# Grouped-query decode block: query-stationary score matmuls, transposed softmax weights, and a rearranged load schedule

## The chip, the cores and the metric

The kernel runs on one core of a Trainium2 chip. The metric is the device time of one execution in microseconds (us), median of several runs. Ratios in this text are the mean time of one kernel's runs over that of the other kernel's runs of the same rounds, with a 95% interval; they are therefore not quite the ratio of the medians quoted next to them. A difference between two variants that were timed in different rounds is a difference of their medians; it is good to some 0.5 us.

## The reference

One decoding step of a transformer block with adaptive layer norm. Batch and query length are 1, the cache holds 65536 positions, and everything is bfloat16.

```python
mod = (silu(c) @ w_mod)                       # 6 x 512: shifts, scales, gates
h = layernorm(x) * (1 + ca) + sa
q = h @ wq                                    # 32 query heads of 128
scores = einsum(q, k) * 128 ** -0.5           # 8 KV heads, 4 query heads share one
p = softmax(scores);  o = einsum(p, v)        # k_cache, v_cache: 8 x 65536 x 128
x = x + ga * (o @ wo)
h = layernorm(x) * (1 + cb) + sb
x = x + gb * ((silu(h @ w_gate) * (h @ w_up)) @ w_down)
```

K and V are 134 MB each. Every byte is used once, so the kernel is a stream of 285.5 MB through one core.

## The kernel before

K and V are loaded in 2 MB chunks of 64 tokens per partition (16 KB per partition), 8 chunks a head, in four K buffers and four V buffers. K loads run 10 chunks ahead of V loads, because V can be used only when a head's softmax is done.

```python
kbuf = ctx.enter_context(tc.tile_pool(name="kbuf", bufs=4))
vbuf = ctx.enter_context(tc.tile_pool(name="vbuf", bufs=4))
LAG = NCH + max(2, NCH // 4)                  # 10 chunks
...
def k_group(g, cidx, j, kt):                  # 8 tokens per partition
    tp = ps_t.tile([P, NPAIR, P], F32, ...)
    for pi in range(NPAIR):                   # two bf16 tokens seen as one fp32 row: 4 transposes
        src = kt[:, t0 : t0 + 2, :].bitcast(F32).rearrange("p a b -> p (a b)")
        nc.tensor.transpose(tp[:, pi, :], src, ident_f[:])
    ktT = ktp.tile([P, NPAIR, P], F32, ...)   # copied by ACT and DVE in turn
    ...
    def emit_s(...):                          # K is the stationary operand
        for pi in range(NPAIR):
            for e in range(2):
                nc.tensor.matmul(sp[:, rep * tl : rep * tl + SN], lhsT=kv[:, :, e], rhs=QB[e][:, g], ...)
...
# softmax of a head: strided max over the free axis, all-reduce over partitions (POOL),
# then four strided exps; only after all four may the head's first V matmul start
...
def v_chunk_start(g, cidx):
    if cidx == 0:
        wo_g = wop.tile([P, rep, D], BF16, ...)
        nc.sync.dma_start(out=wo_g[:], in_=A_wo[...])       # 512 KB in rows of 1 KB
    vt = vbuf.tile([P, CH, Dh], BF16, ...)
    nc.sync.dma_start(out=vt[:], in_=v_src(g, cidx))
...
# after the last V chunk: w_gate, w_up, and w_down in rows of 1 KB, 13/14 of it and then 1/14
```

All large loads are issued by the sync engine (SP) on one queue, in program order; each is spread over the 16 DMA engines.

## Time and profile before

| | before |
|---|---|
| time, median | 688.67 us (687.31 to 689.43, 5 runs) |
| profiled span | 686.9 us |
| input queue (q1) | 285.49 MB, 98.3% of the 16 engines' time |
| PE busy | 524.5 us, 76% |

The page of the kernel before: busy times, then the granted PE clock in tenths and GB/s in 40 equal slices of 17.2 us, then two DMA queues with packets, MB and share of the 16 engines' time.

```profile
span 686.9 us, 17142 instructions
PE 524.5 (76%) x7730; PEld 434.7 (63%) x7730; DVE 253.3 (37%) x420; ACT 194.4 (28%) x324; POOL 12.8 (2%) x40
...
PEclk9999979987999789998999979997899979997555
...
GB/s 350 428 426 405 410 426 429 428 428 421 429 428 428 427 431 426 428 428 425 430 427 430 425 428 432 426 427 424 432 428 427 428 423 430 430 427 424 366 427 192
...
q1 hardware_dynamic: 25488, 285.49, 98.3%
q8 instruction: 60, 0.98, 0.5%
```

The rate is flat near 428 GB/s. The slices below 428 are where to look, and the windows of busy time make them sharper (us from the span's start, length, then busy us of PE, PE weight loads, DVE, ACT and POOL with instruction counts, granted PE clock, DMA share, GB/s):

```profile
60.00:80.00 20.00, 19.36 (x324) 18.82 (x321) 12.85 (x16) 8.91 (x15) 0.00 (x0) 1.00 0.98 394
...
635.00:645.00 10.00, 4.18 (x48) 1.45 (x49) 0.18 (x1) 5.09 (x8) 0.48 (x2) 0.59 0.79 329
...
670.00:680.30 10.30, 5.73 (x137) 4.99 (x135) 2.73 (x15) 0.20 (x2) 0.60 (x1) 0.50 0.81 308
680.30:686.90 6.60, 2.02 (x56) 1.93 (x56) 0.33 (x2) 0.00 (x0) 0.00 (x0) 0.50 0.01 0
```

The largest PE groups (line, engine, operation, out<-in, shapes, count; busy us, mean ns, idle before):

```profile
L268 PE MATMUL tp<-ident_f,k 128*128 128x128 f32 x2048 | 325.5, 294 | 13.4 <-DMA k<-in_A_k_cache_dram 13.3
L283 PE MATMUL sp<-qb,ktT 128*128 128x64 bf16 x4096 | 213.9, 197 | 83.3 <-ACT ktT L273 64.5
...
L316 PE MATMUL oacc<-v,pt 128*16 128x512 bf16 x1024 | 96.0, 410 | 29.1 <-DMA v<-in_A_v_cache_dram 20.9
```

The end of the chain of waits (start, length, what): loads, until the larger piece of w_down lands at 680.25 (the small one lands at 680.55), then all 56 w_down matmuls, then the output.

```profile
628.96 18.77 DMA v<-in_A_v_cache_dram
...
651.09 29.16 DMA wd<-in_B_w_down_dram
680.25 0.05 issue
680.29 2.04 PE pd L422 x56
```

### The profile page before, as it was taken

To read this page: it belongs to the slowest core of one execution; us is meant where nothing else is said; L and a number is where in the kernel's file an instruction comes from. 1 tells how busy PE (TensorE), PEld (TensorE's weight loads), DVE (VectorE), ACT (ScalarE), POOL (GpSimd) and SP (SyncE) were. 2 spreads that over 40 slices of the span, in tenths; PEclk is the share of its full clock that TensorE was granted. 3 is DMA by queue.
4 is the path that set the end of the run, shared out by engine and by line. 5 is a ranking of instruction groups with operands and counts; after the bars stand their busy time and mean duration, and the time that the engine had idled before them with its cause. 6 is when DMAs were issued, how large, how long until landed. Compare 5 with 4: busy or idle time off the path is not lost.

```text
span 686.9 us, 17142 instructions
## 1 busy us (share of the span) xinstructions
PE 524.5 (76%) x7730; PEld 434.7 (63%) x7730; DVE 253.3 (37%) x420; ACT 194.4 (28%) x324; POOL 12.8 (2%) x40
## 2 busy tenths in 40 slices
PE   2699849975999489975998469974999739984344
PEld 2699847864777378864776358863877637772114
DVE  1255714451434234351433324432443514433001
ACT  0144343324233323324232143323232232320200
POOL 1000000000000000000000000000000000000000
PEclk9999979987999789998999979997899979997555
DMA  9999999999999999999999999999999999999895
GB/s 350 428 426 405 410 426 429 428 428 421 429 428 428 427 431 426 428 428 425 430 427 430 425 428 432 426 427 424 432 428 427 428 423 430 430 427 424 366 427 192
DMA packets 25849, 286.58 MB, mean 417 GB/s; under 512 B 2736, under 2 KB 8624, under 8 KB 8624
## 3 DMA queue, kind: packets, MB, share of 16 engines
q1 hardware_dynamic: 25488, 285.49, 98.3%
q8 instruction: 60, 0.98, 0.5%
q14 instruction: 13, 0.11, 0.0%
q10 hardware_dynamic: 288, 0.00, 0.0%
HBM read 285.48 MB, written 0.00 MB: 416 GB/s over the span
## 4 chain that ended last, share of the span: by engine, by line
PE 47%; DMA 27%; issue 13%; DVE 6%; ACT 6%; POOL 1%; SPq 0%; POOLq 0%; ACTq 0%
PE tp L268 25%; DMA v<-in_A_v_cache_dram 15%; PE sp L283 13%; PE oacc L316 7%; DMA k<-in_A_k_cache_dram 7%; DMA wd<-in_B_w_down_dram 4%; ACT pt L238 4%; DVE mx L230 4%; ACT ktT L273 2%; DVE sc L287 1%; PE pa L349 1%; DVE osb L336 1%; DVE oacc L298 0%; SPq L118 0%; DVE ktT L275 0%
## 5 line engine op out<-in xcount | busy, mean ns | idle before, releaser
L268 PE MATMUL tp<-ident_f,k 128*128 128x128 f32 x2048 | 325.5, 294 | 13.4 <-DMA k<-in_A_k_cache_dram 13.3
L283 PE MATMUL sp<-qb,ktT 128*128 128x64 bf16 x4096 | 213.9, 197 | 83.3 <-ACT ktT L273 64.5
L283 PEld LDWEIGHTS <-ktT 128*128 128x128 bf16 x4096 | 186.2, 101 | 129.7 <-ACT ktT L273 67.3
L273 ACT ACTIVATE ktT<-tp 128x512 f32<-128x512 f32 x256 | 153.0, 598 | 381.9 <-PE tp L268 381.9
L268 PEld LDWEIGHTS tp<-ident_f,k 128*128 128x128 f32 x2048 | 234.9, 149 | 26.4 <-issue 23.6
L275 DVE COPY ktT<-tp 128x1024 bf16<-128x1024 bf16 x256 | 176.1, 691 | 148.1 <-PE tp L268 145.8
L316 PE MATMUL oacc<-v,pt 128*16 128x512 bf16 x1024 | 96.0, 410 | 29.1 <-DMA v<-in_A_v_cache_dram 20.9
L287 DVE COPY sc<-sp 128x256 f32<-128x256 f32 x64 | 27.1, 424 | 178.0 <-PE sp L283 178.0
L316 PEld LDWEIGHTS <-pt 128*16 128x16 bf16 x1024 | 25.3, 91 | 53.9 <-issue 30.2
L238 ACT ACTIVATE pt<-sc,nb 128x512 bf16<-128x512 f32 x32 | 40.7, 1422 | 58.1 <-POOL nb L235 58.1
L230 DVE TENSOR_REDUCE mx<-sc 128x4 f32<-128x2048 f32 x8 | 30.4, 3805 | 0.2
L150 PE MATMUL pmod<-scT,wm 128*128 128x1 bf16 x96 | 3.3, 172 | 12.8 <-DVE scT L144 12.8
L233 POOL PARTITION_ALL_REDUCE gmx<-mx x8 | 3.1, 383 | 464.2 <-DVE mx L230 464.2
L150 PEld LDWEIGHTS <-wm 128*128 128x128 bf16 x96 | 3.4, 118 | 12.7 <-DMA wm<-in_w_mod_dram 7.2
L336 DVE COPY osb<-oacc 128x512 f32<-128x512 f32 x7 | 4.8, 692 | 15.8 <-PE oacc L316 15.8
L339 PE MATMUL pT<-ident_f,osb 128*128 128x128 f32 x32 | 6.2, 323 | 5.3 <-DVE osb L336 4.8
L333 DVE COPY osb<-oacc 128x256 f32<-128x256 f32 x1 | 0.4, 425 | 24.7 <-PE oacc L316 24.7
L249 DVE RECIPROCAL linv<-lt 128x4 f32<-128x4 f32 x8 | 1.4, 176 | 21.8 <-POOL lt L247 21.7
L349 PEld LDWEIGHTS <-wo 128*128 128x128 bf16 x128 | 4.9, 118 | 6.5 <-DVE obf L345 6.5
L339 PEld LDWEIGHTS pT<-ident_f,osb 128*128 128x128 f32 x32 | 3.8, 158 | 7.9 <-DVE osb L336 6.3
L349 PE MATMUL pa<-obf,wo 128*128 128x1 bf16 x128 | 5.5, 173 | 4.2 <-DVE obf L345 4.2
L334 ACT ACTIVATE osb<-oacc 128x256 f32<-128x256 f32 x1 | 0.4, 384 | 29.5 <-DVE osb L333 29.5
(66 smaller groups left out, 58.7 us busy)
## 6 DMA issues: line engine op xcount, KB each, us to landing
k<-in_A_k_cache_dram SPq DMA_DIRECT2D x64, 2048.0 KB, 24.4
v<-in_A_v_cache_dram SPq DMA_DIRECT2D x64, 2048.0 KB, 27.7
wq<-in_A_wq_dram SPq DMA_DIRECT2D x2, 2048.0 KB, 17.5
wo<-in_A_wo_dram SPq DMA_DIRECT2D x8, 512.0 KB, 28.5
wm<-in_w_mod_dram SPq DMA_DIRECT2D x2, 1536.0 KB, 8.5
wg<-in_B_w_gate_dram SPq DMA_DIRECT2D x1, 1792.0 KB, 21.4
wu<-in_B_w_up_dram SPq DMA_DIRECT2D x1, 1792.0 KB, 25.2
wd<-in_B_w_down_dram SPq DMA_DIRECT2D x1, 1664.0 KB, 29.2
```

The source lines that it names most:

```text
L150: nc.tensor.matmul(pmod[:, k * DC + cco : k * DC + cco + 1], lhsT=strided_cols(wrow(wm_pieces, cci)[:, k * D : (k + 1) * D], DC, cco), rhs ...
L230: nc.vector.reduce_max(out=mx[:], in_=sc_g[:].rearrange("p (t h) -> p h t", h=rep), axis=AX.X)
L238: nc.scalar.activation(out=pt_th[:, :, h], in_=sc_th[:, :, h], func=AF.Exp, bias=nb[:, h : h + 1], scale=scale, accum_out=lsum[:, h : h + 1],)
L268: nc.tensor.transpose(tp[:, pi, :], src, ident_f[:])
L273: nc.scalar.activation(out=ktT[:], in_=tp[:], func=AF.Identity)
L275: nc.vector.tensor_copy(out=ktT[:].bitcast(BF16), in_=tp[:].bitcast(BF16))
L283: nc.tensor.matmul(sp[:, rep * tl : rep * tl + SN], lhsT=kv[:, :, e], rhs=QB[e][:, g], start=(e == 0), stop=(e == 1))
L287: nc.vector.tensor_copy(out=sc_g[:, c0 * CH * rep : (c0 + SPC) * CH * rep], in_=sp[:, 0 : SPT * rep])
L316: nc.tensor.matmul(oacc[32 * jg : 32 * jg + 4 * rep, :], lhsT=pt_g[:, rep * t : rep * (t + 4)], rhs=vt[:, tl : tl + 4, :], start=(t < RT), ...
L336: nc.vector.tensor_copy(out=osb[:], in_=oacc[:])
L339: nc.tensor.transpose(pT[:, ib, :], osb[:, ib * Dh : (ib + 1) * Dh], ident_f[:])
L349: nc.tensor.matmul(pa[:, cco : cco + 1], lhsT=strided_cols(wo_g[:, hh, :], DC, cco), rhs=o_bf[:, hh : hh + 1], start=(hh == 0), stop=(hh = ...
```

## The change

q becomes the stationary operand of the score matmuls (32 columns, four column tiles next to each other, 512 moving columns), so scores come out head by head on partitions; the softmax then works on contiguous rows, and its weights P are transposed on PE for the V matmuls. Seven of the eight wo loads move into the phase in which only K is loaded. After the last K chunk every second V chunk goes into a freed K buffer. w_down is loaded in 2 KB rows and four pieces. One transpose buffer in PSUM is given up for P. And one small unused tile is added at the top.

```diff
+    pad = const.tile([P, 40], F32, name="pad")
+    nc.gpsimd.memset(pad[:], 0.0)
...
-    wop = ...(name="wop", bufs=2)          # ktp 6, ps_t 4, SLAG 2
+    wop = ...(name="wop", bufs=max(2, Hkv - 1))   # ktp 7, ps_t 3, ps_p 1, SLAG 1
...
-                for e in range(2):
-                    nc.tensor.matmul(sp[:, rep * tl : rep * tl + SN], lhsT=kv[:, :, e], rhs=QB[e][:, g], ...)
+        quad.append((cidx * NG + j, ktT))
+        if len(quad) == 4: ...
+                for e in range(2):
+                    for gidx, ktT_m in members:
+                        nc.tensor.matmul(sp[32 * jg : 32 * jg + 32, :], lhsT=QBk[e][:, g, k, :],
+                            rhs=kv[:, :, :, e], ..., tile_position=(0, 32 * jg))
...
+        nc.vector.reduce_max(out=mx[:], in_=sc_g[:], axis=AX.X)
+        for blk in range(NBLK):
+            nc.scalar.activation(out=p_sb[:], in_=sc_g[:, blk * BW : (blk + 1) * BW], func=AF.Exp, ...)
+            for pp in range(4):
+                nc.tensor.transpose(ptps[:, pp, :], p_sb[:, pp * P : (pp + 1) * P], ident_bf[:])
+            nc.vector.tensor_copy(out=ptT[:, blk], in_=ptps[:])
...
-        vt = vbuf.tile([P, CH, Dh], BF16, name=f"v{g}_{cidx}", tag="vbuf")
+        late = g * NCH + cidx + LAG - Hkv * NCH
+        if late >= 0 and late % 2 == 0:
+            vt = kbuf.tile([P, CH, Dh], BF16, name=f"v{g}_{cidx}", tag="kbuf")
+        else:
+            vt = vbuf.tile([P, CH, Dh], BF16, name=f"v{g}_{cidx}", tag="vbuf")
...
+            if 1 <= step <= Hkv - 1:
+                load_wo(step - 1)            # the eighth follows the last V chunk
...
-        wd_v = B_w_down.rearrange("(c p) n -> p c n", p=P)
+        wd_v = B_w_down.rearrange("(c p e) n -> p c e n", p=P, e=2)
+        for c0, c1 in ((0, 2), (2, 4), (4, 6), (6, FC // 2)):
...
```

## The prediction

> **What bounds the kernel now.** The DMA engines. The page's slice row shows 417 GB/s over the span and about 428 in nearly every slice; the SP queue's 285.5 MB take 98.3% of the 16 engines' time. At 428 GB/s they cost 667 us; about 20 us of the 686.9 us span is not steady streaming. Busy times by window place most of it:
> - 0 to 10 us: 224 and 359 GB/s, 3.2 us lost (the start).
> - 60 to 80 us: 370 to 406 GB/s, 1.6 us lost. Only K is loaded; PE is 97% busy. The chain shows 0.47 (transposes) + 0.23 (scores) = 0.70 us per group of 8 K tiles, 5.6 us a chunk, against 4.9 us for the DMA to bring one.
> - 635 to 645 us: 329 GB/s, 2.3 us lost. The last softmax (max 3.8 us, then nearly 9 us until POOL scales it, four exps 5.1 us) holds the first V matmul until 640; the four V buffers are full.
> - 670 to 680.3 us: 308 GB/s, 2.9 us lost: the skewed end, and w_down in 1 KB rows. 1 KB packets take 46 ns, 16 KB ones 611 ns: 22 against 27 bytes per ns and engine.
> - 680.3 to 686.9 us: 6.6 us without input. The chain shows 2.04 us of w_down matmuls after the last landing, then the output.
>
> In between, the 4+4 buffers absorb the stalls of PE (76% busy), DVE and ACT.
>
> **What the change does.**
> - Scores: q becomes the 32-column stationary operand, four column tiles side by side: 1024 matmuls of 512 columns replace 4096 of 64 with a 128x128 weight load each. The V matmuls have this form already; twelve take 0.76 us in the chain, 0.063 us each. Estimate: 0.13 us per group, not 0.23. The Trainium skill ("TensorEngine Tiling (Array Packing)", Key Properties) says tiles run loads and matmuls in parallel; the 0.063 us agrees.
> - Added: 128 transposes of P, copies, mask algebra. The transposes wait in PE order on the softmax: a stall of about 10 us per head, like ACT's stall today (longest PE wait 10.4 us). The buffers should absorb it.
> - wo loads move into the K-only phase, same bytes; each gives PE 1.5 us of slack there.
> - Late V chunks alternate into freed K buffers: the 635 us starvation goes.
> - w_down in 2 KB rows, four pieces: estimate 0.5 us less DMA; only 8 of 56 matmuls wait for the last piece, 1.7 us less.
> - About a third fewer instructions: the instruction queue (0.5%, 3.5 us of DMA time) shrinks about 1 us.
>
> **On the critical path.** The PE work that shrinks (scores, 214 us busy) is hardly critical. Gain: 1.6 + 2.3 + 0.5 + 1.7 + 1 + 0.4 (smoother end) = 7.5 us, about 1%.
>
> **Prediction:** 681 us, range 677 to 686.5. Faster by over 2%: 3%; within 2%: 94%; slower: 3%. Over 2% needs 674.9, about the floor of 667 + 3 + 5.
>
> **Right if:** PE busy falls to roughly 400 us or less, or its clock does, with DMA still at 428 GB/s in the middle slices; no dip at 60 to 80 us, none after the last K chunk; under 5.5 us from the last landing to the end; the chain of waits mostly DMA.
>
> **Wrong if:** PE, on a lower clock because it idles more, can't catch up after each softmax stall, so that K buffers stay full (slices below 420 repeating every 80 us); three transpose buffers or the quad bursts throttle the K-only phase; the late wo load delays the last head so that gu, not w_down, ends last (today gu is 1.1 us ahead of w_down).

## The result, and the profile after

The changed kernel takes 681.9 us (681.47 to 682.01, 7 runs), the kernel before 688.16 us in the same and earlier rounds (13 runs). The ratio is 0.9906 (0.9896 to 0.9916): about 6.3 us, 0.9%. Executions over 1.5% slower than the fastest of the same kernel are left out of the means.

The page of the changed kernel:

```profile
span 680.2 us, 11269 instructions
PE 504.9 (74%) x4786; PEld 329.5 (48%) x4786; DVE 245.7 (36%) x451; ACT 188.3 (28%) x340; POOL 14.2 (2%) x45
...
GB/s 347 425 419 417 431 431 430 430 430 430 429 427 431 426 429 430 431 429 428 431 430 430 431 428 430 428 430 428 427 429 430 430 431 431 429 429 431 416 424 210
...
q1 hardware_dynamic: 24624, 285.49, 99.0%
q8 instruction: 37, 0.61, 0.3%
```

The dips of 405 and 410 have become 417 and 431, the 366 near the end has become 416, and the plateau stands at 430. PE busy fell by 20 us only, and its mean granted clock went from 0.894 to 0.88. The same windows and groups:

```profile
60.00:80.00 20.00, 19.76 (x160) 12.96 (x159) 9.27 (x14) 7.76 (x13) 0.00 (x0) 1.00 1.02 423
...
630.00:645.00 15.00, 7.92 (x99) 3.92 (x93) 2.81 (x11) 0.43 (x2) 0.44 (x1) 0.73 1.01 415
640.00:645.00 5.00, 1.88 (x16) 0.54 (x16) 0.00 (x0) 0.00 (x0) 0.00 (x0) 0.50 1.00 380
...
664.00:674.60 10.60, 6.61 (x167) 5.89 (x165) 2.72 (x15) 0.18 (x1) 0.60 (x1) 0.50 0.76 308
674.60:680.20 5.60, 1.06 (x24) 0.95 (x24) 0.33 (x2) 0.00 (x0) 0.00 (x0) 0.50 0.02 1
```

```profile
L297 PE MATMUL tp<-ident_f,k 128*128 128x128 f32 x2048 | 289.3, 296 | 73.6 <-DMA k<-in_A_k_cache_dram 45.2
...
L317 PE MATMUL sp<-ktT,qbk 128*32 128x512 bf16 x1024 | 137.3, 419 | 1.6 <-ACT ktT L302 0.3
L375 PE MATMUL oacc<-v,ptT 128*16 128x512 bf16 x1024 | 92.6, 422 | 24.4 <-DMA v<-in_A_v_cache_dram 24.4
```

A small dip remains after the last K chunk, 380 GB/s at 640 to 645 us. It is not starvation: the DMA share is 1.00, and 18 of the 116 packets of 16 KB that start there take 0.8 to 1.4 us in place of 0.61. Why they do is open.

The chain now ends with a wait for w_down and only 24 of its matmuls:

```profile
656.19 18.44 DMA wd<-in_B_w_down_dram
674.63 0.05 issue
674.67 1.07 PE pd L483 x24
```

### Two readings made from the trace's DMA records

GB/s in slices tells an average over 16 engines. Two more readings, worked out from the records of DMA packets and landings, proved more useful.

The first is **when** so many MB of the input queue had been moved (us from the span's start; the ends of the packets, added up):

| MB moved | before | changed | difference |
|---|---|---|---|
| 20 | 50.58 | 51.04 | +0.46 |
| 40 | 99.50 | 98.21 | -1.29 |
| 120 | 287.20 | 285.12 | -2.07 |
| 260 | 615.69 | 611.91 | -3.78 |
| 272 | 646.24 | 639.93 | -6.31 |
| 285.4 | 679.03 | 673.84 | -5.19 |

Each column comes from one profile, and such times scatter. Two variants below, late_v_only and wd_only, run the program of the kernel before without any difference until after the last K chunk; their profiles have 98.84 and 98.34 us at 40 MB and 614.94 and 614.45 us at 260 MB. A lead of about 1 us in a single profile therefore shows nothing.

The second is the **spread**: each load raises its semaphore 16 times, once per DMA engine, so the trace shows when the first and the last of the 16 engines finished a given load. "Last input" is the last landing of any load.

| kernel | instruction packets (q8) | spread near 100 / 300 / 620 us | last input | span | last input to end |
|---|---|---|---|---|---|
| before | 60 | 2.7 / 5.3 / 11.2 | 680.6 | 686.9 | 6.3 |
| changed | 37 | 2.2 / 4.7 / 8.1 | 675.3 | 680.2 | 4.9 |

The engines do not advance together. They drift apart all through the run, to 11 us in the kernel before and to 8 us in the changed one. A load counts as landed when its slowest engine is done, so the engine that is furthest behind decides the end.

### The profile page after: what moved, and what is told of

Same layout as the page of the kernel before. It is cut to its first block, busy times and chain, and to the rows that moved or that the text cites. A ratio compares the mean times of both kernels' runs of the same rounds, so it can differ in the third digit from the quotient of the medians.

```text
span 680.2 us, 11269 instructions
## 1 busy us (share of the span) xinstructions
PE 504.9 (74%) x4786; PEld 329.5 (48%) x4786; DVE 245.7 (36%) x451; ACT 188.3 (28%) x340; POOL 14.2 (2%) x45
## 4 chain that ended last, share of the span: by engine, by line
PE 39%; DMA 37%; issue 12%; DVE 7%; ACT 2%; SPq 1%; POOL 1%; POOLq 0%; DVEq 0%; ACTq 0%
DMA k<-in_A_k_cache_dram 23%; PE tp L297 21%; PE sp L317 9%; DMA v<-in_A_v_cache_dram 9%; PE oacc L375 5%; DMA wq<-in_A_wq_dram 3%; DMA wd<-in_B_w_down_dram 3%; DVE mx L247 2%; DVE ktT L304 2%; PE ptps L269 2%; SPq L424 1%; ACT p L259 1%; ACT sc L331 1%; DVE osb L395 1%; PE pa L408 1%
## 5 line engine op out<-in xcount | busy, mean ns | idle before, releaser
L297 PE MATMUL tp<-ident_f,k 128*128 128x128 f32 x2048 | 289.3, 296 | 73.6 <-DMA k<-in_A_k_cache_dram 45.2
L317 PE MATMUL sp<-ktT,qbk 128*32 128x512 bf16 x1024 | 137.3, 419 | 1.6 <-ACT ktT L302 0.3
L375 PE MATMUL oacc<-v,ptT 128*16 128x512 bf16 x1024 | 92.6, 422 | 24.4 <-DMA v<-in_A_v_cache_dram 24.4
L317 PEld LDWEIGHTS <-qbk 128*32 128x32 bf16 x1024 | 31.8, 95 | 55.7 <-issue 47.5
L375 PEld LDWEIGHTS <-ptT 128*16 128x16 bf16 x1024 | 27.9, 91 | 48.4 <-issue 32.5
L269 PE MATMUL ptps<-ident_bf,p 128*128 128x128 bf16 x128 | 16.2, 266 | 38.3 <-ACT p L259 38.3
L259 ACT ACTIVATE p<-sc,nb 128x512 bf16<-128x512 f32 x32 | 22.9, 716 | 49.5 <-DVE nb L255 45.5
L247 DVE TENSOR_REDUCE mx<-sc 128x1 f32<-128x2048 f32 x8 | 18.3, 2286 | 15.0 <-ACT sc L331 15.0
L270 DVE COPY ptT<-ptps 128x512 bf16<-128x512 bf16 x32 | 13.6, 424 | 25.0 <-PE ptps L269 24.5
L329 DVE COPY sc<-sp 128x512 f32<-128x512 f32 x16 | 11.1, 691 | 16.2 <-PE sp L317 16.2
```

What stands on the lines that cost most here:

```text
L247: nc.vector.reduce_max(out=mx[:], in_=sc_g[:], axis=AX.X)
L259: nc.scalar.activation(out=p_sb[:], in_=sc_g[:, blk * BW : (blk + 1) * BW], func=AF.Exp, bias=nb[:, 0:1], scale=scale, accum_out=lblk[:, b ...
L269: nc.tensor.transpose(ptps[:, pp, :], p_sb[:, pp * P : (pp + 1) * P], ident_bf[:])
L270: nc.vector.tensor_copy(out=ptT[:, blk], in_=ptps[:])
L317: nc.tensor.matmul(sp[32 * jg : 32 * jg + 32, :], lhsT=QBk[e][:, g, k, :], rhs=kv[:, :, :, e], start=(k == 0 and e == 0), stop=(k == 3 and ...
L329: nc.vector.tensor_copy(out=sc_g[:, blk * BW : (blk + 1) * BW], in_=sp[:])
```

## The experiments

Theory A is that of the prediction: the queue is the limit, and the gain is the sum of stretches of lost streaming. Its rival B is that the smaller PE work is the gain. Theories C (the slowest DMA engine) and D (the addresses of the buffers) came from the results.

### The load changes alone

```diff
 the kernel before, with: wo loads early, late V in K buffers, w_down in 2 KB rows and four pieces
```

> The kernel before with only the parts of the change that concern loads: late V chunks alternate into K buffers, wo loaded during the K-only phase, w_down in 2 KB rows and four pieces. Scores and softmax as before. Theory A (the DMA queue is the limit; what counts is lost streaming and the two ends): 3.5 to 5 us faster than before, 683.5 to 684.5 us: 2 us from the end of the starvation after the last K chunk, about 1 us from the tail, the rest from w_down and from the K-only phase, where each wo load gives PE time. Rival B (the smaller PE work is the gain): under 1.5 us faster. PE busy about 524 us as before.

Measured: 685.33 us, ratio 0.9956 (0.9944 to 0.9968), 3.0 us faster. That is just under A's range and above B's. Last input 678.5, span 683.5; 5.0 us from the last input to the end. Spread near 620 us: 11.2, with 60 instruction packets.

### The scores and the softmax alone

```diff
 the changed kernel, with: wo with each head's first V chunk, late V in V buffers, w_down as before
```

> The changed kernel with the three load changes undone: late V in V buffers only, wo loaded with each head's first V chunk, w_down in 1 KB rows and two pieces. New scores and softmax stay. Theory A: 2.5 to 3.5 us faster than before (685 to 686): the dip at 60 to 80 us is gone (1.6), the instruction queue is about 1 us smaller, and the last softmax is a little shorter, so that the dip after the last K chunk shrinks by less than 1 us. Theory B: about 5 to 6 us faster (682 to 683), nearly all of the whole change's 6.3 us.

Measured: 687.61 us, ratio 0.9987 (0.9974 to 1.0000): a gain of 0.9 us, with an interval from 0 to 1.8. Both theories are wrong about it. The page shows where it loses. Its GB/s row starts so:

```profile
GB/s 349 429 428 372 395 424 431 427 421 425 432 430 430 423 431 428 429 429 423 432 433 428 430 425 427 429 431 425 430 429 429 431 425 428 433 429 422 385 428 207
```

The dip in slices 4 and 5, which the prediction meant to remove by cheaper scores, is deeper than before (372 and 395 against 405 and 410). The chain of waits there shows the rhythm of one K chunk:

```profile
54.31 2.53 PE tp L297 x20
56.84 0.86 PE sp L317 x8
57.71 1.04 PE tp L297 x8
...
58.84 0.70 DVE ktT L304
...
59.58 0.88 PE sp L317 x6
60.46 2.53 PE tp L297 x20
```

From 54.31 to 60.46 a chunk takes 6.15 us. The kernel before does one group in 0.70 us, so eight in 5.6 us:

```profile
55.16 0.47 PE tp L268 x4
55.87 0.47 PE tp L268 x4
56.57 0.47 PE tp L268 x4
```

The new form is slower in this phase. Eight score matmuls take 0.86 us, 0.108 us each, not the 0.063 us that the V matmuls gave. The transposes take 0.127 us each in their long bursts, against 0.47 / 4 = 0.117 us. And once per chunk PE waits for the last copied group of K before it can do the second set of scores (0.83 us between 58.75 and 59.58). Which property of the score matmuls makes them slower than the V matmuls (32 against 16 columns, or the moving operand that is read with a stride) was not separated.

### One load change at a time

```diff
 late_v_only (kernel before):
-        vt = vbuf.tile(...)
+        late = g * NCH + cidx + LAG - Hkv * NCH
+        vt = kbuf.tile(...) if late >= 0 and late % 2 == 0 else vbuf.tile(...)
 wo_early_only (kernel before):
+            if 1 <= step <= Hkv - 1: load_wo(step - 1)     # wop: 2 -> 7 buffers
 wd_only (kernel before):
-        wd_v = B_w_down.rearrange("(c p) n -> p c n", p=P)   # two pieces
+        wd_v = B_w_down.rearrange("(c p e) n -> p c e n", p=P, e=2)   # four pieces
```

> The kernel before with one edit: every second V chunk after the last K chunk goes into a K buffer. Theory A: 2.0 us faster than before (the step between 270 and 272 MB delivered), 329 GB/s at 635 to 645 us becomes 420 or more, nothing else changes. Theory B: no effect (within 0.5 us), since PE work is the same.

Measured: 688.03 us, ratio 0.9995 (0.9983 to 1.0007). The starvation is gone, as expected, and the time is not:

```profile
635.00:645.00 10.00, 5.30 (x48) 1.76 (x49) 0.18 (x1) 4.12 (x8) 0.44 (x1) 0.53 1.01 429
...
670.00:680.00 10.00, 5.54 (x144) 5.07 (x144) 2.72 (x15) 0.18 (x1) 0.60 (x1) 0.50 0.55 208
```

329 GB/s at 635 to 645 us became 429, and 308 GB/s at the end became 208. The landings say why. In the kernel before, the V loads of the "starved" stretch land at 633.1, 638.1, 642.9, 647.7 and 652.6 us: every 4.85 us, the full rate. The engine that is furthest behind never starved. Only the engines ahead of it waited, and the spread fell from 9.8 to 3.6 us. Without the starvation the engines ahead stay ahead (spread 11.4 us to the end) and run out of work early, which is the 208 GB/s. The last input lands at 679.9 instead of 680.6 us.

> The kernel before with one edit: the first seven wo loads are issued with K chunks 1 to 7, the eighth after the last V chunk. It gives PE 1.5 us more per chunk in the K-only phase. Expected: the dip at 60 to 80 us goes, 30 MB to 40 MB delivered about 1 us earlier than before, 1.2 to 2.2 us faster in all (686 to 687), nothing of it from PE, whose work is unchanged. If the PE work of the scores is what removes the dip: within 0.5 us of before.

Measured: 687.65 us, ratio 0.9990 (0.9978 to 1.0003). In time that is 0.7 us (interval -0.2 to 1.5), about half of what was expected. The profile is 0.7 us ahead of the kernel before at 32 MB and 1.0 us at 40 MB, as expected; but wd_only, which has no edit that acts there, is 1.0 and 1.2 us ahead in its profile. So this run does not show what the early wo loads do with the old scores.

> The kernel before with w_down in 2 KB rows and four pieces, nothing else. Expected: 1.5 to 2.2 us faster than before, 686.2 to 686.9: 0.5 us less DMA time, and about 1.2 us less from the last landing to the end, because 24 or fewer of the 56 last matmuls wait for the last pieces.

Measured: 687.78 us, ratio 0.9991 (0.9979 to 1.0003), less than half of what was expected. From the last input to the end it takes 5.8 instead of 6.3 us. The packet records give 896 packets of 2 KB at a median of 84 ns where there were 1792 of 1 KB at 46 ns: 4.7 instead of 5.2 us of the 16 engines' time, the 0.5 us expected.

None of the three intervals excludes zero. Their point estimates add up to 1.7 us, and together they gave 3.0 us.

### Late V taken out of the changed kernel

```diff
-        if late >= 0 and late % 2 == 0:
-            vt = kbuf.tile(..., tag="kbuf")
-        else: ...
+        vt = vbuf.tile(..., tag="vbuf")
```

> The changed kernel with the late V chunks back in V buffers alone; everything else as changed. Theory C: the starvation that this brings back idles only the engines that are ahead; the engine that is furthest behind keeps streaming, so under 0.8 us slower (682 to 682.7). The prediction's reckoning (bytes lost on average): 2 us or more slower, 684.

Measured: 683.18 us, ratio 0.9924 (0.9912 to 0.9936), 1.3 us slower than the changed kernel: between the two expectations. The starvation is back:

```profile
630.00:645.00 15.00, 10.43 (x115) 4.54 (x116) 3.65 (x13) 2.40 (x7) 0.44 (x1) 0.78 0.91 371
```

The spread falls from 7.6 to 0.8 us in it, while the loads go on landing every 4.85 to 4.92 us, so here too the engine that is furthest behind did not starve. What is longer comes later: one landing interval is 5.85 us, although all 16 engines are busy from 635 us on and that load had been issued 12 us before. An instruction packet of 0.96 us starts within it, at 649.8 us, and another at 674.65 us, just before the last piece of w_down lands (1.5 us after the third piece, against 0.6 us in the changed kernel). A likely reading is that once the engines are level, the engine that such a packet holds up is at once the last one; it rests on one profile. The same edit was worth 0.35 us in one kernel and 1.3 us in the other, but late V alone has an interval of -0.5 to 1.2 us, so that the two differ is not shown.

### Is PE the limit? Scores twice

```diff
-    scale = float(Dh) ** -0.5
+    scale = 0.5 * float(Dh) ** -0.5
...
+                        for dup in range(2):      # the second copy accumulates
                             nc.tensor.matmul(sp[32 * jg : 32 * jg + 32, :], ...)
```

> The changed kernel with every score matmul issued twice (second copy accumulates, the scale is halved, so the result stays right): score matmuls 1024 to 2048, PE busy rises by up to 130 us at the same clock, to 580 to 640 us of the 680. Theory A: within 1.5 us of the changed kernel (681.5 to 683.5), and any loss lies in the K-only phase before 90 us. Theory B: it takes the gain back or more, 688 us or above.

Measured: 704.74 us (701.41 to 710.23), 22.8 us slower than the changed kernel. The time lies where Theory B expected it, and Theory A's expectation was wrong: PE has less slack than 110 us of extra score matmuls (1024 at 0.108 us).

```profile
PE 586.7 (83%) x5810; PEld 361.6 (51%) x5810; DVE 245.7 (35%) x451; ACT 188.8 (27%) x340; POOL 14.3 (2%) x45
...
GB/s 352 422 419 418 412 430 421 431 429 427 392 406 423 431 425 362 381 430 428 421 328 416 428 429 370 408 428 430 429 373 412 428 429 422 343 430 426 425 415 267
```

Where PE falls behind, the GB/s row has a dip every four to five slices, once per head, and the spread stays below 2 us, because every stall lets the engines catch up with each other. The row of the changed kernel has no such dips, and its spread grows all the time. So does that of the kernel before. In both, PE is not what holds the stream in the middle.

### More PE time with few instructions, and with many

```diff
 pe_few, from the eleventh K chunk on, before the transposes of every second group:
+            nc.tensor.matmul(tp[...], lhsT=ident_bf[:], rhs=QBk[0][...][:, 0:512], ...)   # overwritten
 pe_many, before the transposes of every group:
+            for _ in range(4):
+                nc.tensor.matmul(tp[0:1, 0, 0:1], lhsT=ident_bf[:, 0:1], rhs=ident_bf[:, 0:1], ...)
```

> The changed kernel plus 216 matmuls of 512 columns on PE from the eleventh K chunk on: about 46 us of PE time, but only 432 more instructions (1 to 2 more blocks). Theory C: within 1 us of the changed kernel as long as PE still keeps up (PE slack in the middle is estimated at some 40 us, from the run with doubled scores: 110 us more matmul time, 23 us longer); spread at 620 us about 8 us. If PE no longer keeps up, both pe_few and pe_many are longer and the spread falls to about 2 us, as with doubled scores, and the pair says nothing about fetches.

Measured: 681.79 us, ratio 0.9899 (0.9885 to 0.9914), equal to the changed kernel.

```profile
PE 544.2 (80%) x4990; PEld 348.4 (51%) x5002; DVE 246.1 (36%) x451; ACT 188.1 (28%) x340; POOL 14.3 (2%) x45
```

PE is busier by 39 us than in the changed kernel, busier even than before (524.5), at the same time. That refutes B for the changed kernel: the 20 us of PE time that the change saved buy nothing, from the eleventh K chunk on, where these matmuls were added. In the K-only phase before it PE time does count, as the scores alone showed.

> The changed kernel plus 1728 one-column matmuls on PE (each with its weight load, so about 3456 more PE instructions, 13 more 16 KB blocks on the instruction queue, 37 to about 50) from the eleventh K chunk on, about 50 us of PE time at 29 ns a pair. Theory C (the fetches delay particular DMA engines, the last of them ends the run): spread at 620 us 9 to 10 us instead of 8, and 1.2 to 2 us slower than the run pe_few, which has about the same PE time. Theory B (PE time is what counts): as slow as pe_few within 0.5 us.

Measured: 689.67 us for five runs (685.13 to 693.55; a sixth, 697.24, slow), ratio 1.0014 (0.9980 to 1.0049). The small matmuls cost PE more than the 29 ns assumed (93 us of idle time put down to issue stand before them in their source view), PE fell behind (slices of 362 to 404 GB/s), and the spread near 620 us fell to 1.9 us. As its expectation says, the pair then tells nothing about fetches. This experiment failed.

### More instructions on another engine

```diff
+        for _ in range(12):                       # in each group of K tiles
+            nc.gpsimd.memset(junk[0:1, 0:1], 0.0)
```

> The changed kernel plus 6144 one-element memsets on the idle POOL engine, 12 per group of K tiles: 6144 more instructions, so about 24 more 16 KB instruction blocks to fetch (37 to 61 packets, the 60 of the kernel before), no other work. New theory C: each fetch takes one DMA engine for about 0.93 us, the fetches rotate over 8 of the 16 engines (their durations repeat with period 8), and the engine that is furthest behind ends the run; so 24 more fetches put 3 on each of 8 engines: the spread between the first and the last of the 16 engines at a chunk's landing, 8 us at 620 us in the changed kernel, goes back to about 11 us as before, and the run gets 2 to 2.8 us slower (684 to 684.7). The prediction's reckoning (share of all 16 engines): 1.3 us slower. Rival (fetches cost nothing, they hide): within 0.4 us.

Measured: 1109.15 us. This failed too, and for three reasons. The scheduler placed long rows of memsets ahead of the heads' all-reduces (831 or 832 in a row for five of the eight), and the softmax waited for them:

```profile
DVE nb L256 <- POOL junk L302: 492.3, 7, 78.0
...
q14 instruction: 61, 0.50, 0.1%
```

POOL's instructions come on another queue (q14) in 8 KB packets of about 309 ns, so they are not the fetches in question. And the extra tile moved the K and V buffers off their alignment. It shows nothing about theory C.

### Which DMA engines are late

```diff
         ffn_w["wd"] = pieces
+        for n in (2, 4, 6, 8, 10, 12, 14):
+            pslot = const.tile([P, 16], BF16, name=f"probe{n}")
+            nc.sync.dma_start(out=pslot[0:n, :], in_=...)
```

> The changed kernel plus seven loads of 32 bytes per partition, with 2, 4, 6, 8, 10, 12 and 14 partitions, queued behind the last weights: each runs on as many DMA engines as it has partitions, and its landings show when those engines got that far. Theory C expects the lag to be bound to particular engines, about 8 of 16 late by 4 us or more against the rest; without such a pattern the lag is spread evenly. Time within 0.5 us of the changed kernel.

Measured: 688.82 us (two runs), 7 us slower than the changed kernel, from seven loads of at most 448 bytes. The landings of the last weights run from 673.7 to 682.0 us, eight up to 678.9 and eight from 680.1, but the widest gap lies elsewhere (675.4 to 677.7), so this run does not show two groups. The kernel before does: when a V chunk lands at 607.6 us, eight engines are within 5.1 us of the first and eight are 9.0 to 11.2 us behind it. The loads on few engines did not show late and early ones to be neighbours, so no simple set was found to which less could be given. The time was the surprise: it was lost evenly.

```profile
GB/s 348 419 405 411 418 427 426 426 425 427 426 426 427 426 426 426 426 424 426 426 426 427 426 427 426 426 428 427 426 425 426 426 426 424 426 426 427 428 416 184
```

426 in place of 430, from the beginning, where none of the added loads ran. What differs there is the address of the buffers. Seven added slots of 32 bytes moved K and V buffers from 0 to 224 modulo 256 bytes of their partition (read from the allocation in the compiled program). The change itself adds an unused tile of 160 bytes. That led to the next run.

### Without the unused tile

```diff
-    pad = const.tile([P, 40], F32, name="pad")
-    nc.gpsimd.memset(pad[:], 0.0)
```

> The changed kernel without its one unused tile (160 bytes per partition, named pad, written once and never read): the K, V and weight buffers then start at 96 modulo 256 bytes of their partition instead of at 0. Theory D (from the run named probe, whose buffers stood at 224 modulo 256): K and V packets of 16 KB take 612 to 621 ns instead of 611, 1% less DMA rate in every slice, 5 to 8 us slower than the changed kernel, 687 to 690 us: most or all of the gain gone. Rival (the probe's small loads or their issue made it slow, not the address): within 0.5 us of the changed kernel, packets at 611 ns.

Measured: 687.2 us (687.14 to 687.31), ratio 0.9981 (0.9969 to 0.9993). Without the tile 5.3 of the 6.3 us are gone.

```profile
GB/s 349 422 404 412 421 427 427 427 427 428 425 427 428 426 426 428 426 426 426 428 427 427 427 428 426 427 426 427 426 428 426 427 426 426 427 427 427 426 419 186
```

The packet records between 110 and 600 us: a 16 KB packet takes 611 ns in nearly all cases in the changed kernel (mean 613.1). Without the tile most take 612 to 622 ns (mean 615.9), in the probe 612 to 621 ns (mean 617.1). In the kernel before the buffers happen to start at 0 modulo 256 as well, so the tile does not speed anything up. It keeps the buffers at 0, where the other new tiles would have moved them; without it the run is 5.3 us, 0.8%, longer. By the packet records the 16 engines are then busy 680.0 instead of 675.9 us on average. The 1 KB packets and the instruction packets are longer as well (means of 48.9 against 46.1 ns and 1063 against 928 ns), and the tile moves everything that is allocated after it. That the load buffers' own address is what counts is therefore likely, not separated.

## Why the prediction was right or wrong

The time was right: 681.0 predicted, 681.9 measured, and "within 2%" at 94%. That the queue is the limit held in every run. The sum of 7.5 us was near the 6.3 us measured, but several of its terms were not what they were said to be. That the time fitted so well was partly luck: errors of the terms cancelled, and without the unused tile, to which the prediction gave no value, 687.2 us would have lain above its range (677 to 686.5).

- **"1.6 us at 60 to 80 us", cheaper scores.** The dip went. The step that failed is "Estimate: 0.13 us per group, not 0.23". Scores cost 0.22 us per group (two sets of 0.87 us per eight groups), and a chunk takes PE 6.15 instead of 5.6 us. The new scores alone made the dip deeper: they reach 40 MB at 101.11 us, 2.9 us after the changed kernel (98.21), which differs from them in this phase by the early wo loads. So these removed the dip of the new scores. The prediction named this help but booked the gain to the scores. Whether anything was gained over the kernel before (99.50) is open, since single profiles of the same work differ by about 1 us there.
- **"PE busy falls to roughly 400 us or less, or its clock does".** It did not: 504.9 us, clock 0.88 against 0.894. Nor is the chain of waits mostly DMA (37%, PE 39%). The conclusion drawn, that the PE work is hardly critical, holds all the same after the K-only phase: 39 us of added PE work cost nothing there.
- **"2.3 us" for the starvation at 635 us.** Read off an average over 16 engines. It was worth 0.35 us (not distinguishable from zero) alone and 1.3 us within the change, because the engine furthest behind did not starve. This is the step whose idea of the mechanism was wrong.
- **"1.7 us" from four pieces of w_down.** The third and fourth piece land at 674.6 and 675.3 us, and 24 matmuls, not 8, are done after the third. From the last input to the end: 6.3 before, 4.9 after, 1.4 us; of the chain, 6.6 before and 5.6 after, 1.0 us.
- **"0.5 us" for 2 KB rows.** Right: 0.5 us of DMA time.
- **"0.4 us (smoother end)".** Absent. The end is as uneven as before, 308 GB/s in both windows.
- **"about 1 us" from fewer instructions.** q8 went from 60 to 37 packets, 3.5 to 2.1 us of the 16 engines' time by the packet records, so 1.3 us on average. It is probably worth more. With the new load schedule, old scores give 685.33 us and new ones 681.9 us, 3.4 us less; the last input moves from 678.5 to 675.3 us, and the spread near 620 us from 11.2 to 8.1 us. PE time is not the cause, as pe_few shows, and the two are level at 40 MB. Each q8 packet occupies an engine for about 0.93 us, and the packets' durations repeat in a cycle of eight, which suggests that eight of the 16 engines take turns; 23 packets fewer would then be 23 / 8 x 0.93 = 2.7 us on each of these. The five kernels with old scores that were profiled (60 packets) have spreads of 10.5 to 11.8 us near 620 us; those with new scores that do not stall (37 to 39 packets) have 6.7 to 8.7. This fits, and the packet and landing records carry it further (engines are told apart only by the order in which they land; stretch of 110 to 600 us). Each q8 packet is followed by a 16 KB packet that takes 1.10 instead of 0.61 us, so that a fetch holds its engine up by 1.4 us. In the kernel before, chunks during which a fetch falls land on the later eight engines 1.6 us later in sum than the rhythm of 4.84 us, chunks without one 0.15 us; on the earlier eight it is 0.35 us in both cases. (In the changed kernel it is 1.3 and 0.3 us, and on the earlier eight 0.5 and 0.3.) And the later eight fall behind the first engine by 7.4 to 7.9 us in the five kernels with old scores (44 or 45 fetches there), by 4.6 to 4.8 us in the four with new scores and buffers at 0 that keep up (27 to 29 fetches); 17 fetches at 1.4 us over eight engines would be 3.0 us. So the traces tie the lag of eight engines to the fetches, by time and by size. What stays an inference is that this is the whole of the 3.4 us: both attempts to add fetches alone failed.
- **Not in the prediction at all: the unused tile.** It was in the diff, and no cost or purpose was given to it. Without it the gain would have been about 1.4 us instead of 6.3 (688.56 against 687.2 us, same rounds).
- **Parts are not additive.** Load changes alone 3.0 us, scores alone 0.9, together 6.3. The scores alone pay in the K-only phase what the wo loads would have hidden (2.0 us behind at 30 MB). A starvation that remains lets the late engines catch up, which would take value from every other repair; this is a reading of the spreads and was not tested.

No tested variant beat the changed kernel.

## What to carry to other kernels

When 16 DMA engines share every load, find the engine that is furthest behind from the first and last landing of each load, and do not count a dip in the average rate as lost time before that engine is seen to wait. Look at what every new tile does to the start address of the load buffers: a few bytes of scratch moved a streaming kernel by 0.8%. Measure the cost of a matmul form in the form itself: the neighbour with the same output width was 1.7 times cheaper (0.063 against 0.108 us).

## What the Trainium skill lacked or had wrong

- "DMA: Bandwidth & Descriptors", section "How a descriptor splits into AXI transactions", says that a transaction must start at a 256-byte boundary and that a descriptor which does not start there costs additional beats. This agrees in direction for 16 KB packets into the on-chip buffers: 611 ns at 0 modulo 256, a mean of 615.9 ns at 96 and 617.1 ns at 224, and 5.3 and 7 us in the time. The page's words are about bytes that are read, and its examples stop at 576 bytes; here the start of the destination was moved, and the source was the same.
- "Runtime: NRT & Kernel Launch", section "Instruction fetch mechanics", says that instructions are refilled in 16 KiB blocks of 256 and calls the cost mostly hidden. The blocks agree (60 and 37 packets of 16 KB on q8, here with 17142 and 11269 instructions). In a kernel bound by loads each occupies a DMA engine for about 0.93 us, the 16 KB packet after it takes 0.49 us longer, and the kernels with fewer of them have less spread between engines (8.1 against 11.2 us). Another queue, q14, brought POOL's instructions in 8 KB packets. The page mentions neither.
- The pages know of slower engines and say that the slowest one sets the pace of a load, but none describes how the 16 engines drift apart in a long stream, here by up to 11 us in 620, or that a stall brings them together again (9.8 to 3.6 us).
- "DMA: Bandwidth & Descriptors", section "Specifications", gives 512 bytes as the smallest transfer at line rate. Here 1 KB packets took 46 ns and 2 KB packets 84 ns, 22 and 24 bytes per ns and engine, against 27 for 16 KB (611 ns).
- "TensorEngine Tiling (Array Packing)", section "Key Properties", says that tiles work in parallel. The V matmuls agree (0.063 us for 512 columns); the score matmuls with 32 columns took 0.108 us, and the page does not say what would set the two apart.
